# Sliding-window attention followed by an MLP: attention of four heads per visit, in 32-row and 32-column tiles of TensorE

## The chip, the cores and the metric

The kernel runs on one core of one Trainium2 chip. The metric is the device time of one execution in microseconds (us); the figure for a kernel is the median of its runs. TensorE is called PE in the profile, VectorE DVE, ScalarE ACT, GpSimd POOL and SyncE SP.

## What is computed

```python
B, H, S, D = 8, 8, 576, 64; window = 64
scores = q @ k.T / sqrt(D)                    # per batch and head
mask = (rel >= 0) & (rel < window)            # rel = query position - key position
attn = exp(scores - max) / sum, masked; O = attn @ v
x = O of all heads side by side: 4608 tokens x 512
h = x @ w_in (512 x 2048); g = h * sigmoid(h); out = g @ w_out (2048 x 512)
```

Inputs and output are float32 in DRAM; the kernel computes in bf16 with float32 sums. Every query sees at most 64 keys, so a block of 64 queries needs 128 keys: its own block and the one before.

## The kernel before

The 4608 tokens are 72 blocks of 64, nine in each batch, and 9 MLP tiles of 512 tokens. For a tile the first layer (L440) makes 16 blocks of 128 hidden channels, each from four matmuls of 512 columns into one of four PSUM banks `mp`; ACT applies silu (L446) into `g`. The second layer (L449) makes four output blocks of 128 tokens, each from 16 matmuls; ACT or DVE copies them out (L455) and SP stores them (L459).

Attention works on pairs of heads and three blocks at a time: 96 groups, twelve in each batch. `qbd` holds q transposed, the two heads of a pair block-diagonally, so that one matmul with 128 rows of k makes the scores of both heads (`scores`, L349; 3 matmuls of 128 columns). ACT takes the exponential (`expo`, L367), DVE multiplies by a 0/1 mask (`masking`, L370), `values` (L375) multiplies by v with a column of ones for the sum, DVE takes reciprocals (L381) and normalises (L387, L404, L410). O must then be turned so that channels lie on partitions (`bridge`). In the first batches PE does this (`back_both` L420, `back` L431) with a copy (`to_bridge` L436); later DMA does (`turn_o`, L425). q and k are turned by PE in the first batches (`turn_heads` L299, `turn_twos` L308, copied by `lift_q` L321, `lift_k` L327, `lift_twos` L314), later by DMA transposes (`turn_rows` L260) with `spread_q` (L268) for q. `load_v` (L272) loads v for blocks 0 to 127, 128 to 255 and so on; `shift_v` (L335, L337) makes the copy that is shifted by 64 rows. Attention has the four PSUM banks `at`; two buffers each hold q, k and v of a batch.

The order of instructions on each engine is fixed before the kernel runs by the class `Plan`. It plays the program with a duration for each step, and each engine takes the ready step of the lowest rank. MLP matmuls have rank 99, so PE does attention whenever it is ready and MLP matmuls in between; `scores_may_run` holds scores back to the second layer. Idle PE time ahead of the first MLP matmul is filled with matmuls on `ident` (L680). SP carries the first two loads of q and k, the DMA transposes and the stores; POOL carries all other loads.

Of the kernel before, what the change touches and what calls it, by code (L numbers as in the profile page):

```python
# [14 lines left out]
class Plan:  # L15
# [5 lines left out]
    def __init__(self, pools, rank, rank0, ahead):  # L21
        self.rank, self.rank0, self.pools = rank, {**rank0, **{c + "0": r for c, r in ahead.items()}}, pools
        self.queues = {}
        self.banks = [[] for _ in range(8)]
        self.count = 0
        self.now = 0.0

    def add(self, cls, us, fn, deps=(), lat=0.08, gate=None, dma=None, pool=None, table=None, b=0):
        if b > 1 and cls in ("cast", "lift", "spread", "mask", "norm"):
            lat = 0.2  # L30
        op = dict(us=us, first=self.rank[cls] + b if b or cls not in self.rank0 else self.rank0[cls], fn=fn, deps=[d for d in deps if d is not None], lat=lat, gate=gate, dma=dma,
                  pool=pool, table=table, seen=None, n=self.count, until=[], bank=None)
        self.count += 1
        self.queues.setdefault(cls, []).append(op)
        return op

    def add_filler(self, n, cls, us, fn, *args, **kw):

        for _ in range(n):
            op = self.add(cls, us, None, *args, **kw)  # L40
            op["until"], op["fn"] = [op], lambda e, op=op: fn(op)
        self.count -= n

# [3 lines left out]
    def run(self):  # L47
# [4 lines left out]
        table, left = "exp", self.count  # L52
        pipe = {True: 0.0, False: 0.0}
        events, order = [0.0], []
        while left:
# [6 lines left out]
            while moved:  # L62
                moved = False
                for e in engines:
# [3 lines left out]
                    for c in can[e]:  # L68
                        q = self.queues[c]
                        if head[c] == len(q):  # L70
                            continue
                        op = q[head[c]]
                        if e not in op["us"] or (best and best[0]["first"] <= op["first"]):
                            continue
                        if not self.done(op["deps"]) or (op["gate"] and not op["gate"]()):
                            continue
                        if op["pool"] and not any(self.done(self.banks[i]) for i in self.pools[op["pool"]]):
                            continue
                        best = (op, c)
# [3 lines left out]
                    if op["pool"]:  # L83
                        banks = self.banks
                        op["bank"] = min((i for i in self.pools[op["pool"]] if self.done(banks[i])),
                                         key=lambda i: max([u["seen"] for u in banks[i]], default=0.0))
                        banks[op["bank"]] = op["until"]
                    head[c] += 1
                    us = op["us"][e]
                    if op["table"] and op["table"] != table:  # L90
                        table, us = op["table"], us + 1.28
                    end = free[e] = now + us
                    if op["dma"] is None:
                        op["seen"] = end + op["lat"]
                    else:

                        soft = e == "POOL"
                        begin = max(pipe[soft], end + 0.9)
                        pipe[soft] = begin + op["dma"] * (1.25 if soft and pipe[False] > begin else 1.0)
                        op["seen"] = pipe[soft] + 2.2 + (0.0 if now < 40 else 6.0 if soft else {"xk": 5.0, "xo": 1.0}.get(c, 0.0))  # L100
                    op["at"], op["cls"], op["by"] = now, c, e
                    order.append((op, e))
                    left -= c != "warm"
                    moved = True
                    heapq.heappush(events, end)
                    heapq.heappush(events, op["seen"])
        for op, e in order:
            op["fn"](e)
# [3 lines left out]
def kernel(ctx, tc, q, k, v, w_in, w_out, out):  # L112
# [4 lines left out]
    NP = H // 2  # L117
    NB = S // 64
    NM = 6
    NR = S // NM  # L120
    NG = 3
    NDC = d_model // 128
    NFT = d_ff // 128
    TT = 512
    NTT = B * S // TT
    TB = TT // 64
    NK = 2
    NN, NNB, NE, NOB, NOT, NGT = 8, 8, 14, 6, 4, NFT + 3
    PARTS = {0: [(0, 192), (192, TT)]}
    NXQ, NXK, NXO = 4, 2, 3  # L130
    NRAW, NOX, NRC = 2, 2, 12
    NIV, NPM = 2, 1
    scale = 1.0 / float(D) ** 0.5


    ctx.enter_context(tc.manual_schedule())

# [3 lines left out]
    ident = keep.tile([128, 128], BF16, name="ident")  # L141
    twoi = keep.tile([128, 64], BF16, name="twoi")
    zero = keep.tile([128, NP], FP32, name="zero")
    spare = keep.tile([128, NP], FP32, name="spare")
    window = keep.tile([128, 64], BF16, name="window")
    mask0 = keep.tile([128, 3, 2, 64], BF16, name="mask0")
    mask = keep.tile([128, 3, 2, 64], BF16, name="mask")
    bias0 = keep.tile([128, 3, 2, 64], BF16, name="bias0")
    bias = keep.tile([128, 3, 2, 64], BF16, name="bias")
    nats = [keep.tile([NR, 2, NM, 128], BF16, name=f"nat{i}") for i in range(NN)]  # L150
    natbs = [keep.tile([NR, 2 * NM * D], BF16, name=f"natb{i}") for i in range(NNB)]
    qbd = [keep.tile([128, NP, 2, S], BF16, name=f"qbd{i}") for i in range(NK)]
    kt = [keep.tile([128, 64 + NP * S], BF16, name=f"kt{i}") for i in range(NK)]
    vv = [keep.tile([128, H * NB + 1, D + 2], BF16, name=f"vv{i}") for i in range(NK)]
    es = [keep.tile([128, 3, 2, 64], BF16, name=f"e{i}") for i in range(NE)]
    rcs = [keep.tile([128, 3, 2], FP32, name=f"rc{i}") for i in range(NRC)]
    obs = [keep.tile([128, 3, 128], BF16, name=f"ob{i}") for i in range(NOB)]
    raws = [keep.tile([128, 2, S], BF16, name=f"raw{i}") for i in range(NRAW)]
    oxs = [keep.tile([128, 3, NP, 128], BF16, name=f"ox{i}") for i in range(NOX)]
    gts = [keep.tile([128, TT], BF16, name=f"g{i}") for i in range(NGT)]  # L160
    ots = [keep.tile([128, d_model], FP32, name=f"ot{i}") for i in range(NOT)]
    bridge = keep.tile([128, B * NB, NDC, 64], BF16, name="bridge")
    w_in_sb = keep.tile([128, NDC, d_ff], BF16, name="w_in_sb")
    w_out_sb = keep.tile([128, NFT, d_model], BF16, name="w_out_sb")
    banks = [psum.tile([128, 512], FP32, name=f"at{i}") for i in range(4)]
    banks += [psum.tile([128, 512], FP32, name=f"mp{i}") for i in range(4)]

    p = Plan(
        {"at": range(4), "mp": range(4, 8), "all": range(8)},
        rank=dict(prime=-8, one=-9, first=-9, dma=-1, ld0=-1, ld1=-1, st=-2, xo=-1.5, xk=-1.4, silu=-3, out=-2, pv=0, ot=0, s=1, moe=99, warm=200, turn=2,  # L170
                  norm=0, inverse=0, bridge=0, exp=1, mask=1, lift=2, spread=2, shift=2, cast=4, late=5, clear=9),
        rank0=dict(turn=-6, cast=-6, lift=-5, shift=-4.5, exp=-4, mask=-4, inverse=-3.5, norm=-3, bridge=-3.2),
        ahead=dict(s=-5.5, exp=-4.6, pv=-5.5, inverse=-4.3, norm=-4.2, ot=-5.5, bridge=-4.25),
    )
    copies = {"ACT": nc.scalar.copy, "DVE": nc.vector.tensor_copy, "POOL": nc.gpsimd.tensor_copy}
    queue = {"SP": nc.sync, "ACT": nc.scalar, "POOL": nc.gpsimd}


    def const_ident(_):
        nc.gpsimd.memset(ident, 0.0)  # L180
        nc.gpsimd.affine_select(out=ident, in_=ident, compare_op=ALU.not_equal, fill=1.0,
                                base=0, channel_multiplier=1, pattern=[[-1, 128]])

    def const_window(_):

        nc.gpsimd.memset(window, 0.0)
        nc.gpsimd.affine_select(out=window, in_=window, compare_op=ALU.is_ge, fill=-32768.0,
                                base=-1, channel_multiplier=1, pattern=[[-1, 64]])
        nc.gpsimd.affine_select(out=window, in_=window, compare_op=ALU.is_ge, fill=-32768.0,
                                base=64, channel_multiplier=-1, pattern=[[1, 64]])  # L190

    def const_bias(_):
        for t in (bias, bias0):
            nc.vector.tensor_copy(out=t.rearrange("p t h i -> p (t h) i"),
                                  in_=window.unsqueeze(1).to_broadcast([128, 6, 64]))
        nc.vector.memset(bias0[0:64, 0], -32768.0)

    def const_mask(_):
        for a, m in ((bias, mask), (bias0, mask0)):
            nc.vector.tensor_scalar(m, a, 1.0 / 32768.0, 1.0, op0=ALU.mult, op1=ALU.add)  # L200

    def const_twoi(_):
        nc.vector.tensor_copy(out=twoi[0:64], in_=ident[0:64, 0:64])
        nc.vector.tensor_copy(out=twoi[64:128], in_=ident[64:128, 64:128])

    def clear_vv(i):
        nc.vector.memset(vv[i][:, :, D:D + 1], 1.0)
        nc.vector.memset(vv[i][0:64, 0, 0:D], 0.0)

    def clear_k(i):  # L210
        nc.vector.memset(kt[i][:, 0:64].bitcast(FP32), 0.0)

    def clear_q(i, hh):
        r = slice(64 - 64 * hh, 128 - 64 * hh)
# [35 lines left out]
    def rows(i):  # L250
        return nats[i]
# [484 lines left out]
```

## Time and profile before

| | |
|---|---|
| runs | 315.54, 315.95, 319.11 us; median 315.95 |
| profiled execution: span | 318.8 us; of the three runs 319.11 fits this span |
| PE busy | 307.9 us (97%), 2198 matmuls |
| DVE, ACT, POOL busy | 154.5, 193.4, 119.2 us |
| first MLP matmul | starts at 22.1 us |
| software DMA (POOL's queue) | 95712 packets, 18.06 MB |
| hardware DMA (SP's queue) | 42368 packets, 19.08 MB |

A span runs from the first to the last instruction. A line of the timeline gives start, duration, engine, line, operation, tiles written and read, shape and count; lines that overlap on PE are pipelined matmuls, so the distance between the starts of two lines is what the first of them cost. In the view by stages each engine has its busy time and, in brackets, its instructions; then come the granted TensorE clock, the busy share of the DMA engines and the rate of the bytes written. A line of the chain gives start, duration and what the time was spent on.

### The profile page before, as it was taken

To read this page: it belongs to the slowest core of one execution; us is meant where nothing else is said; L and a number is where in the kernel's file an instruction comes from. 1 tells how busy PE (TensorE), PEld (TensorE's weight loads), DVE (VectorE), ACT (ScalarE), POOL (GpSimd) and SP (SyncE) were. 2 spreads that over 40 slices of the span, in tenths; PEclk is the share of its full clock that TensorE was granted. 3 is DMA by queue.
4 is the path that set the end of the run, shared out by engine and by line. 5 is a ranking of instruction groups with operands and counts; after the bars stand their busy time and mean duration, and the time that the engine had idled before them with its cause. 6 is when DMAs were issued, how large, how long until landed. Compare 5 with 4: busy or idle time off the path is not lost.

```text
span 318.8 us, 6010 instructions
## 1 busy us (share of the span) xinstructions
PE 307.9 (97%) x2198; PEld 168.4 (53%) x2223; DVE 154.5 (48%) x467; ACT 193.4 (61%) x374; POOL 119.2 (37%) x159
## 2 busy tenths in 40 slices
PE   8999999999999999999999869999999999999996
PEld 4778666545664556445544445446544444444444
DVE  4894748934799898923990159606920000000000
ACT  8898786889776565568356721668166126415611
POOL 8947859496829777564454000000000000000000
PEclk9999999999999999999999979999999999999999
DMA  9999999999999999999999933400340020020012
GB/s 144 164 196 186 193 195 161 127 243 129 187 165 135 176 154 152 163 163 163 154 191 175 142 64 90 84 0 36 80 93 2 35 97 0 2 99 33 2 61 70
DMA packets 138108, 37.51 MB, mean 118 GB/s; under 512 B 122464, under 2 KB 133600, under 8 KB 138080
## 3 DMA queue, kind: packets, MB, share of 16 engines
q0 software_dynamic: 95712, 18.06, 74.4%
q1 hardware_dynamic: 42368, 19.08, 33.6%
q8 instruction: 17, 0.28, 0.4%
q14 instruction: 11, 0.09, 0.1%
HBM read 36.70 MB, written 9.44 MB: 145 GB/s over the span
## 4 chain that ended last, share of the span: by engine, by line
PE 85%; DVE 6%; DMA 4%; issue 2%; ACT 1%; POOL 1%; DVEq 0%; POOLq 0%; ACTq 0%
PE mp L449 36%; PE mp L440 32%; PE at L375 5%; PE at L349 4%; DMA vv<-in_v_dram 4%; DVE qbd L314 2%; PE at L680 1%; PE mp L680 1%; DVE ox L404 1%; POOL vv L272 1%; DVE qbd L268 1%; DVE vv L337 1%; DVE vv L335 1%; PE at L308 1%; PE at L420 1%
## 5 line engine op out<-in xcount | busy, mean ns | idle before, releaser
L449 PE MATMUL mp<-w_out_sb,g 128*128 128x512 bf16 (+2 forms) x583 | 141.6, 369 | 1.0
L440 PE MATMUL mp<-bridge,w_in_sb 128*128 128x512 bf16 (+2 forms) x640 | 130.7, 358 | 0.7 <-ACT g L446 0.6
L446 ACT ACTIVATE g<-mp 128x512 bf16<-128x512 f32 (+2 forms) x160 | 86.3, 556 | 29.8 <-PE mp L440 29.3
L440 PEld LDWEIGHTS <-w_in_sb 128*128 128x128 bf16 x640 | 60.1, 98 | 60.3 <-issue 1.4
L449 PEld LDWEIGHTS <-g 128*128 128x128 bf16 x608 | 55.0, 98 | 42.7
L455 ACT COPY ot<-mp 128x512 f32<-128x512 f32 (+2 forms) x34 | 19.0, 561 | 72.1 <-PE mp L449 62.7
L404 DVE TENSOR_TENSOR ox<-at,rc 64x192 bf16<-64x192 f32 x128 | 45.2, 353 | 2.5
L254 POOL DMA_DIRECT2D nat<-in_k_dram x48 | 36.4, 761 | 24.3 <-DMA nat<-in_k_dram 13.0
L367 ACT ACTIVATE e<-at 128x384 bf16<-128x384 f32 x90 | 38.8, 497 | 10.6 <-PE at L349 9.8
L370 DVE TENSOR_TENSOR e<-e,mask 128x384 bf16<-128x384 bf16 x84 | 26.6, 350 | 33.6 <-ACT e L367 32.8
L272 POOL DMA_DIRECT2D vv<-in_v_dram x32 | 32.3, 1014 | 13.1 <-PE at L375 7.2
L375 PE MATMUL at<-vv,e 128*128 128x130 bf16 x273 | 29.8, 220 | 4.1 <-DVE e L370 4.0
L375 PEld LDWEIGHTS <-e 128*128 128x128 bf16 x288 | 22.5, 97 | 20.0 <-DVE e L370 7.6
L254 POOL DMA_DIRECT2D nat<-in_q_dram x32 | 23.4, 735 | 8.1 <-DMA nat<-in_q_dram 4.6
L349 PEld LDWEIGHTS <-kt 128*128 128x128 bf16 x252 | 18.6, 100 | 10.0 <-issue 2.8
L349 PE MATMUL at<-qbd,kt 128*128 128x128 bf16 x252 | 23.6, 222 | 0.3
L381 DVE RECIPROCAL rc<-at 128x6 f32<-128x6 f32 x91 | 17.5, 194 | 10.1 <-PE at L375 8.0
L314 DVE COPY qbd<-at 64x288 bf16<-64x288 bf16 x26 | 12.5, 480 | 11.1 <-ACT qbd L314 7.6
L387 DVE TENSOR_TENSOR ob<-at,rc 64x192 bf16<-64x192 f32 x40 | 14.0, 350 | 0.8
L314 ACT COPY qbd<-at 64x288 bf16<-64x288 bf16 x22 | 10.5, 476 | 2.8 <-DVE qbd L314 2.5
L268 DVE COPY qbd<-raw 64x1152 bf16<-64x1152 bf16 x16 | 8.1, 505 | 8.4 <-DMA raw<-nat 8.0
L235 POOL DMA_DIRECT2D natb<-in_q_dram x15 | 10.0, 665 | 4.9 <-PE at L375 1.4
(69 smaller groups left out, 158.0 us busy)
## 6 DMA issues: line engine op xcount, KB each, us to landing
out_dram<-ot SPq DMA_DIRECT2D x35, 256.0 KB, 2.4
vv<-in_v_dram POOLq DMA_DIRECT2D x32, 144.0 KB, 7.3
nat<-in_k_dram POOLq DMA_DIRECT2D x48, 72.0 KB, 7.9
nat<-in_q_dram POOLq DMA_DIRECT2D x32, 72.0 KB, 7.6
natb<-in_q_dram POOLq DMA_DIRECT2D x15, 144.0 KB, 6.4
w_in_sb<-in_moe_w_in_dram POOLq DMA_DIRECT2D x8, 256.0 KB, 8.7
w_out_sb<-in_moe_w_out_dram POOLq DMA_DIRECT2D x8, 256.0 KB, 7.8
natb<-in_k_dram POOLq DMA_DIRECT2D x7, 144.0 KB, 5.9
```

The source lines that it names most:

```text
L254: nc.gpsimd.dma_start(out=rows(i)[:, pj % 2, :, 64 * hh:64 * hh + 64], in_=(q, k)[kk][b, 2 * pj + hh].rearrange("(m p) d -> p m d", p=NR),)
L272: queue[e].dma_start(out=vv[b % NK][:, 2 * g0 + 1:2 * g1 + 1:2, 0:D], in_=v[b].rearrange("h s d -> (h s) d").rearrange("(g p) d -> p g d", ...
L314: copies[e](out=qbd[b % NK][64 * hh:64 * hh + 64, pj, hh].rearrange("x (p m) -> x p m", m=NM)[:, :, r::2], in_=at_bf16(op)[64 * r:64 * r + ...
L349: nc.tensor.matmul(at_sp(op)[:, x], lhsT=kt[b % NK][:, pj * S + t * 64:pj * S + t * 64 + 128], rhs=qbd[b % NK][:, pj, :, t * 64:t * 64 + 6 ...
L367: nc.scalar.activation(out=es[n % NE], in_=at_sp(op), func=ACTF.Exp, scale=scale)
L370: nc.vector.tensor_mul(es[n % NE], es[n % NE], mask0 if g == 0 else mask)
L375: nc.tensor.matmul(at_pv(op)[:, x], lhsT=es[n % NE][:, x].rearrange("p h i -> p (h i)"), rhs=vv[b % NK][:, s:s + NB + 1:NB, 0:D + 1], star ...
L404: nc.vector.tensor_mul(ox(n)[:, :, r], pv[r, :, hh, 0:D], rc[r, :, hh:hh + 1].to_broadcast([64, 3, 64]))
L440: nc.tensor.matmul(banks[bank["bank"]][:, lo:hi], lhsT=w_in_sb[:, c, ft * 128:(ft + 1) * 128], rhs=bridge[:, (j * TT + lo) // 64:(j * TT + ...
L446: nc.scalar.activation(out=gts[gt][:, lo:hi], in_=banks[bank["bank"]][:, lo:hi], func=ACTF.Silu)
L449: nc.tensor.matmul(banks[bank["bank"]][:, 0:hi - lo], lhsT=gts[gt][:, m * 128:(m + 1) * 128], rhs=w_out_sb[:, f, lo:hi], start=(f == 0), s ...
L455: copies[e](out=ots[ot][:, lo:hi], in_=banks[bank["bank"]][:, 0:hi - lo])
```

## The change

Attention is written anew; the MLP keeps its shape. Four heads are handled at once, one in each quarter of the 128 partitions. Within a quarter, a 32-partition strip holds 32 of the head's 64 channels at a time: a row of q or k is seen as 32 words of two bf16 numbers, and DVE turns 32x32 blocks of such words (`turn`). The channel pairs then lie next to each other, and scores sum over the two members (`r`) in two matmuls with 32 rows each, at row tile 32j for head j, each head into a PSUM bank of its own. `values` takes 32 queries as weights, at column tile 32j, so that 32 queries of four heads fill the 128 partitions of a bank. After reciprocal and `norm`, DVE turns 32x32 blocks of O straight into `bridge` (`cross`), which has its channels in a new order; `load_w_in` loads w_in's rows in that order. All transposes on PE and by DMA go.

A visit is the attention of up to eight blocks for one group of four heads (`quad`): 64 matmuls for scores, two exps and two masks, 64 matmuls for values, reciprocal, norm, cross. It uses four PSUM banks at once (`A`), first for the scores, then for the values. The nine blocks of batch 0 are done ahead of the MLP in four smaller visits (blocks 0 to 3 and 4 to 8 of each group), with all eight banks. After that the two visits for tile j+1 are placed within the second layer of tile j (`may_score`). The first layer's first two pieces have 256 and 320 columns. q and k of batch 0 come as float32 in 16 loads on SP and are cast by ACT and DVE; all other loads are on POOL, with three buffers for q, k and v. The planner is a shorter one with new ranks and durations. Parts of the diff (the removed functions are those printed above):

```diff
-    banks = [psum.tile([128, 512], FP32, name=f"at{i}") for i in range(4)]
-    banks += [psum.tile([128, 512], FP32, name=f"mp{i}") for i in range(4)]
+    half = [psum.tile([128, 4, 512], FP32, name="at"), psum.tile([128, 4, 512], FP32, name="mp")]
...
+        {"A": [(0, 1, 2, 3)], "AD": [(0, 1, 2, 3), (4, 5, 6, 7)], "D": [(i,) for i in range(4, 8)],
+         "any": [(i,) for i in range(8)]},
+        rank=dict(one=-9, cast=-2, turn=2, shift=3, scores=-1, exp=0, mask=1, values=-2, inverse=-1, norm=0, cross=0.5,
+                  prime=-8, silu=-3, out=4, moe=99, warm=200, load=0, first=0, st=1),
+        rate=0.37,
...
+    def rows(x, b, h):
+        return x[b, h].rearrange("(t p m) d -> p t (m d)", p=32, m=2)
+    def load_wide(i, x, quad, j):
+        nc.sync.dma_start(out=wide[i][32 * j:32 * j + 32], in_=rows(x, 0, 4 * quad + j))
+    def load_rows(w, x, b, quad, j):
+        nc.gpsimd.dma_start(out=raws[w][32 * j:32 * j + 32], in_=rows(x, b, 4 * quad + j))
+    def load_v(b, i):
+        n = min(128, S - 128 * i)
         nc.gpsimd.dma_start(
+            out=vas[b % NK][0:n, i, :, 0:D], in_=v[b, :, 128 * i:128 * i + n].rearrange("h p d -> p h d"))
...
+    def turn(w, b, quad, kk, lo, hi):
+        t = kts[b % NK][:, quad, 64:] if kk else qts[b % NK][:, quad]
+        nc.vector.transpose(
+            out=t.rearrange("x s c -> x (s c)").bitcast(FP32)[:, 64 * lo:64 * hi].rearrange("x (t p m) -> x t m p", p=32, m=2),
+            in_=raws[w][:, lo:hi].rearrange("p t y -> p (t y)").bitcast(FP32).rearrange("p (t m x) -> p t m x", m=2, x=32))
+
+    def shift_v(e, b, up):
+        a, z = vas[b % NK], vbs[b % NK]
+        if up:
+            copies[e](out=z[64:128, :, :, 0:D], in_=a[0:64, :, :, 0:D])
...
+    def scores(op, quad, blocks):
+        ps = half[op["bank"][0] // 4]
+        for s, g in enumerate(blocks):
+            b, t = divmod(g, NB)
+            for r in range(2):
+                for j in range(4):
+                    x = slice(32 * j, 32 * j + 32)
+                    nc.tensor.matmul(
+                        ps[:, j, 64 * s:64 * s + 64], lhsT=kts[b % NK][x, quad, 64 * t:64 * t + 128, r],
+                        rhs=qts[b % NK][x, quad, 64 * t:64 * t + 64, r], start=(r == 0), stop=(r == 1),
+                        tile_position=(32 * j, 0))
+    def expo(op, n, j0, j1, nb):
+        nc.scalar.activation(out=es[n % NE][:, j0:j1, 0:64 * nb], in_=half[op["bank"][0] // 4][:, j0:j1, 0:64 * nb],
+                             func=ACTF.Exp, scale=scale)
+    def masking(n, j0, j1, nb):
+        t = es[n % NE][:, j0:j1, 0:64 * nb].rearrange("k j (s i) -> k j s i", i=64)
+        nc.vector.tensor_mul(t, t, mask.unsqueeze(1).unsqueeze(1).to_broadcast([128, j1 - j0, nb, 64]))
+    def values(op, n, quad, blocks):
+        ps = half[op["bank"][0] // 4]
+        for s, g in enumerate(blocks):
+            b, t = divmod(g, NB)
+            vv = (vas if t % 2 else vbs)[b % NK][:, t // 2]
+            for a in range(2):
+                for j in range(4):
+                    x = slice(32 * j, 32 * j + 32)
+                    c = (2 * (s % 2) + a) * (D + 1)
+                    nc.tensor.matmul(
+                        ps[x, s // 2, c:c + D + 1], lhsT=es[n % NE][:, j, 64 * s + 32 * a:64 * s + 32 * a + 32],
+                        rhs=vv[:, 4 * quad + j, 0:D + 1], start=True, stop=True, tile_position=(0, 32 * j))
...
+    def norm(op, n, nb):
+        for lo, hi, ps in pieces(op, nb):
+            kk = ps.shape[1]
...
+    def cross(n, quad, g0, nb):
+        nc.vector.transpose(
+            out=bridge[:, 2 * quad:2 * quad + 2, 64 * g0:64 * (g0 + nb)].rearrange("x c (u i) -> x c u i", i=32),
+            in_=obs[n % NO][:, 0:2 * nb].rearrange("i u (x c) -> i c u x", c=2))
...
+        op, kind, rest = moe[may_score.i]
+        return (kind == 1 and rest == NF * NC and not p.done(op["deps"])) or (kind == 2 and rest > 8)
...
+        s = p.add("scores", {"PE": 0.1 + 0.11 * nb}, None, need, lat=0.15, pool="AD" if early else "A",
+                  gate=None if early else may_score)
...
+        for j0, j1 in ([(0, 4)] if early else [(0, 2), (2, 4)]):
+            ex = p.add("exp", {"ACT": 0.2 + 0.000834 * 64 * nb * (j1 - j0)}, lambda _, j0=j0, j1=j1: expo(s, n, j0, j1, nb),
+                       [s] + e_free.get(n - NE, []), table="exp")
+            ma.append(p.add("mask", {"DVE": 0.16 + 0.00053 * 64 * nb * (j1 - j0)}, lambda _, j0=j0, j1=j1: masking(n, j0, j1, nb),
+                            [ex, c_mask]))
+            exps.append(ex)
+            s["until"].append(ex)
+        va = p.add("values", {"PE": 0.1 + 0.11 * nb}, None, ma + [x for g in blocks for x in v_done[g]], lat=0.15,
+                   pool="AD" if early else "A")
...
+        rc = p.add("inverse", {"DVE": 0.25}, lambda _: inverse(va, n, nb), [va])
+        no = p.add("norm", {"DVE": 0.2 + 0.134 * nb}, lambda _: norm(va, n, nb), [rc] + o_free.get(n - NO, []))
+        va["until"].append(no)
+        cr = p.add("cross", {"DVE": 0.1 + 0.134 * nb}, lambda _: cross(n, quad, blocks[0], nb), [no])
+        o_free[n] = [cr]
...
+    for quad in range(2):
+        for lo, hi in FIRST:
+            add_visit(quad, list(range(lo, hi)), early=True)
+    add_qk(1)
+    add_v(1)
...
+    add_first([(64 * lo, 64 * hi) for lo, hi in FIRST], "any")
+    loaded = 1
+    for j in range(NT):
+        if j + 1 < NT:
+            lo = NB if j == 0 else 8 * (j + 1)
+            blocks = list(range(lo, 8 * (j + 2)))
+            while loaded < blocks[-1] // NB:
+                loaded += 1
+                add_qk(loaded)
+                add_v(loaded)
+            for quad in range(2):
+                add_visit(quad, blocks)
+        add_second(j)
+        if j + 1 < NT:
+            add_first([(64 * blocks[0], 64 * blocks[-1] + 64)], "D")
```

## The prediction

> **What bounds the kernel now.** I read the busy shares first, then the chain of work that ended last, then busy time by stage, then the timeline of TensorE (PE).
>
> ```profile
> PE 307.9 (97%) x2198; PEld 168.4 (53%) x2223; DVE 154.5 (48%) x467; ACT 193.4 (61%) x374; POOL 119.2 (37%) x159
> ...
> PE 85%; DVE 6%; DMA 4%; issue 2%; ACT 1%; POOL 1%; DVEq 0%; POOLq 0%; ACTq 0%
> ```
>
> PE is 97% busy and is 85% of the chain, so a microsecond of PE work is a microsecond of time wherever nothing else is late. The long pieces of the chain give the price of the MLP:
>
> ```profile
> 131.69 13.81 PE mp L440 x64
> ...
> 171.67 12.93 DMA vv<-in_v_dram
> ...
> 260.39 13.81 PE mp L440 x64
> ...
> 302.10 13.64 PE mp L449 x94
> ```
>
> 64 matmuls of 512 columns take 13.81 us, 215.8 ns each; the 1152 of both layers take 248.6. Smaller pieces of the first tile and of the last store add 0.6: 249.2. They start at 22.1 and end near 315.5, and the store ends the span at 318.8. So 318.8 = 22.1 (opening) + 249.2 + 3.3 (tail) + 44.2 (all else). The DMA line is part of that: v of a late batch lands at 184.6, and PE sits idle:
>
> ```profile
> 185.99 0.51 PE L375 MATMUL at<-vv,e 128*128 128x130 bf16 x3 [4.00 <-DVE e L370]
> ...
> 178.00:201.00 23.00, 18.83 (x120) 10.17 (x122) 14.05 (x45) 7.83 (x16) 0.00 (x0) 0.93 0.68 93
> 215.00:233.00 18.00, 17.84 (x131) 10.13 (x132) 13.36 (x45) 8.66 (x18) 0.00 (x0) 1.00 0.27 67
> ```
>
> The last two lines are the same stage (second layer plus its attention groups) with and without the late v; the third figure from the right is the granted TensorE clock. It is 0.93 of full in the first: after the idle 4.0 us, 0.07 x 23 = 1.6 us more were lost to a lower clock. So 5.6 of the 44.2 is this stall and 38.6 is attention on PE: scores and values of 84 groups about 28 (0.17 us for three matmuls each), transposes of q, k and O about 7, small waits the rest.
>
> **Its own time.** The three runs are 315.54, 315.95 and 319.11. A span of 318.8 fits only the last, 0.3 more than the span; the median is 3.2 below it, so I take it that the stall is smaller in the others.
>
> **What goes.** The PE transposes and their evacuations, the DMA transposes of q, k and O, and the diagonal layout of q go: about 7 us of PE between 22 and 62. DMA gets lighter: 80 loads of 576 packets become 32 to 33 thousand packets of twice the size, and all transposing packets (most of the 42368 hardware ones) go. Three buffers instead of two hold k and v. I therefore count the v stall at nothing; the cover is that a batch is loaded in some 12 us of DMA (10 thousand packets, at the 9 to 10 thousand per 10 us moved here between 70 and 120) out of a 35 us stretch. POOL issues 16 loads x 0.73 and 5 x 1.01 = 17 us per batch, also inside 35. If that cover failed, the 5.6 would be back.
>
> **What PE gets.** A visit (8 blocks, 4 heads) has two PE stages, scores and values, of 64 matmuls each with 64 or 65 moving columns, as 16 sets of four tiles. 63 blocks x 2 head groups / 8 = 15.75 visits lie after the opening. The nearest rows:
>
> ```profile
> 20.64 0.38 PE L420 MATMUL mp<-ident,ox 128*64 128x64 bf16 x12
> 20.95 0.35 PE L375 MATMUL at<-vv,e 128*128 128x130 bf16 x3
> 21.22 0.28 PE L420 MATMUL mp<-ident,ox 128*64 128x64 bf16 x6
> 21.44 0.34 PE L375 MATMUL at<-vv,e 128*128 128x130 bf16 x3
> ...
> 46.54 0.25 PE L431 MATMUL at<-twoi,ob 128*128 128x64 bf16 x3
> 46.63 0.38 PE L449 MATMUL mp<-w_out_sb,g 128*128 128x512 bf16 x1
> ```
>
> L420 works in pairs of 64-column tiles. Twelve take 20.95 - 20.64 = 0.31 us, six take 0.22: three more pairs cost 0.09, so a pair costs 30 ns, as much as one full-width matmul of L431 (0.09 / 3). Two column tiles thus do run side by side. The rest, 0.22 - 0.09 = 0.13, is the way out of the tile shape; the way in shows as 0.26 before L420 at 14.15 where three matmuls take 0.17: 0.09. Together 0.21 per stage, hidden by nothing.
>
> Four tiles, and row tiles at all, no row shows. Below: a set goes like a pair, 30 ns. Above: it goes like two pairs, 60 ns, which is also 8 instructions at the 7.5 ns that the pair shows. I take the middle, 45, since the pair is near both: a stage is 0.21 + 16 x 0.045 = 0.93, a visit 1.86, all 29.3 us (21.7 to 37.0 at the ends). Before, a steady second-layer stage with its groups takes 17.1 (from 146.0 to 163.1); after it is 13.8 + 4 x 0.93 = 17.5. The steady tile gains nothing; the gain is the transposes, the stall, and that q, k and O need no PE in the first three tiles.
>
> The Trainium skill's page "TensorEngine Tiling (Array Packing)", section Restrictions and Gotchas, speaks against this: column tiles lose the fast weight load. With an estimate from "TensorE: Matmul & The Clock Gate", section LDWEIGHTS (columns / 1.2 ns), four 32-column loads in a row would be 107 ns a set and the sum some 16 us higher. L420's loads are tiled too, and its pair still costs 30 ns, so I go by the row.
>
> **What DVE and ACT get.** ACT: 512 columns take 0.60, 192 take 0.31, so 1024 (half a visit's exp) take 1.06. DVE: PSUM multiplies of 384 and 192 columns take 0.541 and 0.353, 0.98 ns an element and 0.17 fixed; a norm of 1024 is 1.17. A mask of 384 takes 0.350, so 1024 take 0.66. The 32x32 transpose has no row. Below, a dense copy: 1152 in 0.51. Above, the dearest DVE element here, 353 / 192 = 1.84 ns: 1.9 for 1024. I take one element per 0.98 ns, as any unaided DVE pass here: cross 1.17, a turn of 576 words 0.73. Per tile of 31 us DVE gets some 12 and ACT 18, so neither is the bound by its sum.
>
> **The chain inside a tile.** Both visits of the next tile must end within one second-layer stage, because one PSUM half carries both stages of both. From its start: scores to 0.9; last silu and table load to 2.0; two exps to 4.1; mask 4.9; values 5.1 to 6.0; reciprocal 6.4; norm 7.7; scores of the second visit 7.9 to 8.8; exps 11.1; mask 11.9; values 12.0 to 13.0; reciprocal 13.3; norm 14.6; cross 15.9. PE reaches the first layer at 17.5, so 1.6 are spare. Where a step is late, PE stands at values or at the first layer's first matmul, the MLP matmuls queued behind wait with it, and silu and the stores wait for those. The order is fixed ahead at 0.98 us for a stage, so a quicker PE comes early to values and waits; I give 2 us in all.
>
> **Opening.** SP issues 16 loads of q and k at 0.41 from 0.74, until 7.3; five v loads (1.01 each) start once the first k has landed, about 5.3. That is 3.5 MB of reads at 0.30 to 0.38 MB per us (the first and second 10 us here): v lands near 13.5. Two shifts (0.79 and 0.86 now for 2304) to 15.2; values 0.7; then reciprocal, norm and cross of three small visits, 5.2 us of DVE, before both head groups have blocks 0 to 3: 21.5 to 22.5. I take 22.0 (19 to 25): nothing gained on 22.1. Casts and turns come before v lands.
>
> **Sum.** 22.0 + 249.2 + 29.3 + 2.0 + 3.3 = 305.8 span, 306.1 with the 0.3. That is 13 below the profiled run and 3.1% below the median of 315.95. About 2% (309.6 to 322.3) is what a measurement here can tell from no change.
>
> **Rivals.** (1) The chain outlasts the stage. If transposes cost 1.9 and the broadcast mask goes at 0.98 ns an element (1.17), and a turn stands in the way once per visit, the chain is 3 us longer: 1.4 over in each of 8 stages, 11 us, and with the 2 already counted 315. It decides from 1.6 us on. For it: one PSUM half, single visits in flight; against: DVE is idle for most of the first-layer stage, where turns fit. The page "VectorE: DVE Perf Modes", section The three transpose paths, gives 311 ns for a 128x128 bf16 transpose; scaled, an estimate of 2.5 for a cross, it would add 1.3 to the chain, just inside the spare time. No run here shows it.
> (2) Slower: tiles do not overlap in one of the stages. Row tiles write four PSUM banks at once and read every second element; no row shows either. At 30 ns a matmul the stage is 0.21 + 1.92 = 2.13; for scores alone 15.75 x 1.20 = 19 more, 325; for both, 344. It decides at 2.9 us a visit, 77 ns a set. Against: L420's pairs.
> (3) Better: 30 ns a set and no waits, 22.0 + 249.2 + 21.7 + 3.6 = 296.5.
>
> **How the numbers follow.** Forecast with its own range 297 to 313: 0.67 (0.58 of it under 309.6). Rival 1: 0.14 (0.02 faster, 0.10 within 2%, 0.02 slower). Rival 2: 0.13, all slower. Rival 3 exactly or below: 0.03. A late opening or a new DMA wait of 5 us or more: 0.03, within 2%. That makes faster 0.63, same 0.22, slower 0.15. The range 297 to 321 leaves out rival 2 and the best cases, under 2 in 10.
>
> **What would show it.** Right: both PE stages at 0.7 to 1.2 us with sets of four starting within nanoseconds; first MLP matmul near 22; tiles 31 to 32 us apart; no wait of PE for v. Wrong: single matmuls 30 ns apart in the tiled stages; PE waiting at the first layer for cross; DVE transposes well above 1.2 us; a first MLP matmul after 25.

## The result, and the profile after

The changed kernel takes 469.69 us (four runs, 466.74 to 473.14) against 316.23 for the kernel before: a ratio of 1.486, 95% interval 1.474 to 1.497. The forecast was 306.1 with a range of 297 to 321. The kernel got slower by half where it was to get a little faster, and the forecast was 163.6 us too low. (Some executions of the kernel before last about 5 us longer than its others; medians are over all runs, ratios and intervals are those on record, and against the shorter executions of before alone, 314.8 to 317.9, the ratios of e1 and of e5 to e9 below would be 0.005 to 0.015 higher.)

The page of the changed kernel, its span being 467.1 us: busy time, the granted TensorE clock in 40 slices (9 is full speed), and the chain that ended last by engine and by line. L275 and L288 are the two MLP layers, L283 is silu, L292 the copy out. The last line is that of the first layer in the table of groups: busy us, mean ns of one, and after the second bar the time that PE idled before these matmuls and what ended most of it.

```profile
PE 324.7 (70%) x3588; PEld 150.0 (32%) x3631; DVE 115.8 (25%) x179; ACT 161.2 (35%) x244; POOL 115.4 (25%) x175
...
PEclk9799999799999999999999999999769999999999
...
PE 61%; ACT 23%; DMA 6%; issue 6%; POOL 2%; DVE 1%; another core or an unknown queue 1%; ACTq 0%; DVEq 0%; POOLq 0%
PE mp L275 30%; PE mp L288 24%; ACT gate L283 18%; ACT ot L292 4%; DMA va<-in_v_dram 4%; PE at L288 3%; DMA w_in_sb<-in_moe_w_in_dram 2%; PE at L275 2%; PE at L223 2%; PE at L245 1%; POOL va L187 1%; DVE ot L292 1%; POOL raw L183 1%; ACT L283 1%
...
L275 PE MATMUL mp<-bridge,w_in_sb 128*128 128x512 bf16 (+3 forms) x552 | 144.6, 380 | 93.1 <-ACT gate L283 86.1
```

PE fell from 97% to 70% busy, and ACT, which was 1% of the chain, is 23%. It does less work than before (161.2 us against 193.4), yet it ends waits: 18% of the span is silu. No engine is the bound by its sum. The view of waits says who stands for whom (total us, times, longest):

```profile
PE mp L275 <- ACT gate L283: 86.1, 128, 0.9
...
PE mp L288 <- ACT ot L292: 11.7, 17, 0.7
```

One stage in the timeline shows the pattern (start, duration, engine and line; in brackets the idle time before and what ended it):

```profile
338.24 1.86 PE L275 MATMUL mp<-bridge,w_in_sb 128*128 128x512 bf16 x4 [0.68 <-ACT gate L283]
340.79 1.86 PE L275 MATMUL mp<-bridge,w_in_sb 128*128 128x512 bf16 x4 [0.68 <-ACT gate L283]
...
347.68 0.60 ACT L283 ACTIVATE gate<-mp 128x512 bf16<-128x512 f32 x1 [1.84 <-PE mp L275]
348.33 1.02 PE L275 MATMUL mp<-bridge,w_in_sb 128*128 128x512 bf16 x4 [0.68 <-ACT gate L283]
349.39 0.60 ACT L283 ACTIVATE gate<-mp 128x512 bf16<-128x512 f32 x1 [1.11 <-PE mp L275]
350.03 1.02 PE L275 MATMUL mp<-bridge,w_in_sb 128*128 128x512 bf16 x4 [0.69 <-ACT gate L283]
351.09 0.60 ACT L283 ACTIVATE gate<-mp 128x512 bf16<-128x512 f32 x1 [1.11 <-PE mp L275]
```

PE and ACT take turns: four matmuls, 1.06 us later silu, 0.60 for silu, 0.05 to the next matmul. A group takes 1.71 us (350.03 - 348.33 is 1.70) where four matmuls at 215.8 ns make 0.86. There are four banks, so a group should wait only for silu of the group four earlier; here it waits for the group just before. The first two lines are the same at half the granted clock (0.50 from 333.7 to 347.4): 2.55 us a group.

Summed over the trace, from the start of each MLP piece to the start of PE's next work, the MLP takes some 400 us: 252 in the first layer, 148 in the second. The prediction had 249.2 for both. That is some 151 too much, nearly the whole miss of 161.3 in the span (467.1 - 305.8).

### The profile page after: what moved, and what is told of

Same layout as the page of the kernel before. It is cut to its first block, busy times and chain, and to the rows that moved or that the text cites. A ratio compares the mean times of both kernels' runs of the same rounds, so it can differ in the third digit from the quotient of the medians.

```text
span 467.1 us, 8158 instructions
## 1 busy us (share of the span) xinstructions
PE 324.7 (70%) x3588; PEld 150.0 (32%) x3631; DVE 115.8 (25%) x179; ACT 161.2 (35%) x244; POOL 115.4 (25%) x175
## 2 busy tenths in 40 slices
DMA packets 86275, 29.50 MB, mean 63 GB/s; under 512 B 72672, under 2 KB 81760, under 8 KB 86240
## 4 chain that ended last, share of the span: by engine, by line
PE 61%; ACT 23%; DMA 6%; issue 6%; POOL 2%; DVE 1%; another core or an unknown queue 1%; ACTq 0%; DVEq 0%; POOLq 0%
PE mp L275 30%; PE mp L288 24%; ACT gate L283 18%; ACT ot L292 4%; DMA va<-in_v_dram 4%; PE at L288 3%; DMA w_in_sb<-in_moe_w_in_dram 2%; PE at L275 2%; PE at L223 2%; PE at L245 1%; POOL va L187 1%; DVE ot L292 1%; POOL raw L183 1%; ACT L283 1%
## 5 line engine op out<-in xcount | busy, mean ns | idle before, releaser
L275 PE MATMUL mp<-bridge,w_in_sb 128*128 128x512 bf16 (+3 forms) x552 | 144.6, 380 | 93.1 <-ACT gate L283 86.1
L288 PE MATMUL mp<-w_out_sb,gate 128*128 128x512 bf16 (+1 forms) x514 | 116.3, 369 | 22.1 <-ACT ot L292 11.7
L283 ACT ACTIVATE gate<-mp 128x512 bf16<-128x512 f32 (+3 forms) x141 | 80.9, 574 | 146.5 <-PE mp L275 139.4
L275 PEld LDWEIGHTS <-w_in_sb 128*128 128x128 bf16 x640 | 63.1, 99 | 190.1 <-issue 144.6
L288 PEld LDWEIGHTS <-gate 128*128 128x128 bf16 x608 | 56.2, 97 | 82.2 <-issue 23.4
L234 DVE TENSOR_TENSOR e<-e,mask 128x1024 bf16<-128x1024 bf16 (+2 forms) x36 | 24.8, 688 | 132.2 <-ACT e L229 132.0
L187 POOL DMA_DIRECT2D va<-in_v_dram x40 | 34.8, 888 | 71.7 <-PE at L245 70.8
L229 ACT ACTIVATE e<-at 128x1024 bf16<-128x1024 f32 (+1 forms) x33 | 31.6, 1008 | 30.4 <-PE at L223 30.3
L292 ACT COPY ot<-mp 128x512 f32<-128x512 f32 (+1 forms) x27 | 15.2, 562 | 74.3 <-PE mp L288 48.0
L183 POOL DMA_DIRECT2D raw<-in_k_dram x56 | 34.0, 622 | 16.5 <-DVE rc L259 10.1
L183 POOL DMA_DIRECT2D raw<-in_q_dram x56 | 34.8, 633 | 11.5 <-DMA va<-in_v_dram 5.6
L269 DVE STREAM_TRANSPOSE bridge<-o 128x1024 bf16<-128x1024 bf16 (+3 forms) x20 | 22.4, 1124 | 0.4
L275 PE MATMUL at<-bridge,w_in_sb 128*128 128x256 bf16 (+1 forms) x76 | 12.4, 285 | 7.0 <-ACT gate L283 6.4
L288 PE MATMUL at<-w_out_sb,gate 128*128 128x512 bf16 (+1 forms) x63 | 12.7, 352 | 2.2 <-ACT ot L292 2.1
```

The lines of the kernel that those rows point to most:

```text
L183: nc.gpsimd.dma_start(out=raws[w][32 * j:32 * j + 32], in_=rows(x, b, 4 * quad + j))
L187: nc.gpsimd.dma_start(out=vas[b % NK][0:n, i, :, 0:D], in_=v[b, :, 128 * i:128 * i + n].rearrange("h p d -> p h d"))
L229: nc.scalar.activation(out=es[n % NE][:, j0:j1, 0:64 * nb], in_=half[op["bank"][0] // 4][:, j0:j1, 0:64 * nb], func=ACTF.Exp, scale=scale)
L234: nc.vector.tensor_mul(t, t, mask.unsqueeze(1).unsqueeze(1).to_broadcast([128, j1 - j0, nb, 64]))
L269: nc.vector.transpose(out=bridge[:, 2 * quad:2 * quad + 2, 64 * g0:64 * (g0 + nb)].rearrange("x c (u i) -> x c u i", i=32), in_=obs[n % NO ...
L275: nc.tensor.matmul(bank(bk["bank"][0])[:, 0:hi - lo], lhsT=w_in_sb[:, c, ft * 128:(ft + 1) * 128], rhs=bridge[:, c, lo:hi], start=(c == 0) ...
```

## The experiments

**Theory A.** The cause is the line `half = [psum.tile([128, 4, 512], ...), psum.tile([128, 4, 512], ...)]`. Four banks are one tile there, and waits are kept for the tile as a whole: whoever writes one bank waits for the reader of another. In the order of the program 152 of the 159 first-layer groups that follow another lie in the same tile as it, and none in the same bank. The rivals: attention is what takes the time (tiles that don't overlap, a visit's chain that is too long), or the loads, or the banks themselves, or the stretches at half clock.

**e1_banks.** The second half is four tiles of one bank each; nothing else of the method changes. Early visits, which also use these banks, take one exp and one norm per bank there.

```diff
-    half = [psum.tile([128, 4, 512], FP32, name="at"), psum.tile([128, 4, 512], FP32, name="mp")]
+    half = psum.tile([128, 4, 512], FP32, name="at")
+    single = [psum.tile([128, 512], FP32, name=f"mp{i}") for i in range(4)]
...
-         "any": [(i,) for i in range(8)]},
+         "any": [(i,) for i in range(4, 8)]},
```

Expected:

> The changed kernel with one edit: the second PSUM half is four tiles of one bank each instead of one tile of four banks (early visits that use it take one exp and one norm per bank), and the first MLP pieces keep to these four. Theory A: waits are kept per tile, so a first-layer group in one bank waits for the silu of the group before in another bank; then the 144 waits of 0.6 us on silu go, a first-layer stage falls from some 27 us to 14, a second-layer stage loses its waits on the copies, and the time falls by about 150 us: opening 36 + MLP 249 + visits 26 + tail and waits 7 = 318 (308 to 330). Rival B: four banks are too few beside visits that hold the other four, and the waits are for the bank's own reader: no change, 455 to 475. Rival C: the granted clock at half for some 30 us is the cause: no change either, since nothing of the clock is edited.

Measured: 313.07 us (four runs, 311.99 to 315.45), ratio 0.983 (0.971 to 0.995). Its page, busy time and the two MLP groups (busy, mean ns, and after the second bar the idle time before them):

```profile
PE 294.8 (94%) x3623; PEld 149.0 (47%) x3623; DVE 116.3 (37%) x184; ACT 159.9 (51%) x246; POOL 115.8 (37%) x175
...
L297 PE MATMUL mp<-w_out_sb,gate 128*128 128x512 bf16 (+2 forms) x608 | 129.7, 368 | 0.0
L284 PE MATMUL mp<-bridge,w_in_sb 128*128 128x512 bf16 (+3 forms) x640 | 126.8, 358 | 0.0
```

The 93.1 us that PE idled ahead of the first layer (the line of L275 above) are 0.0. One line of allocation is 157 us. With it mended the new attention is no slower than the old: beside e1's 311.99 to 315.45, six runs of the kernel before took 315.08 to 317.85, so the gain is nearer 1% than the 1.7% of the ratio.

**e2_before_one.** The converse, in the kernel before: only its four MLP banks become one tile.

```diff
-    banks += [psum.tile([128, 512], FP32, name=f"mp{i}") for i in range(4)]
+    mp = psum.tile([128, 4, 512], FP32, name="mp")
+    banks += [mp[:, i] for i in range(4)]
```

Expected:

> The kernel before with one edit: its four mp banks are one tile of four banks. Theory A: each first-layer group (0.86 us) now also waits for the silu before it (0.6) and two hand-overs of some 0.1: 0.8 x 144 = 115 us more, and the second layer's first matmul waits for a copy (0.6 + 0.2, 36 times, part of it hidden): 430 to 470 in all. Rivals B and C: the banks and their number are as before: 316.

Measured: 509.01 us (502.35 and 515.68), beyond the range. The first layer's group in this kernel's table of groups:

```profile
L441 PE MATMUL mp<-bridge,w_in_sb 128*128 128x512 bf16 (+2 forms) x640 | 176.0, 400 | 104.0 <-ACT g L447 97.7 <-ACT ot L456 5.2 <-DVE ot L456 0.8
```

The stall is the same with the old attention: 97.7 us of waiting for silu. It needs nothing of the new attention. The surplus over the expectation stands beside two things that the expectation left out: a longer time at half clock, 88.2 us of this span of 500.6 (openings included) against 33.1 in the changed kernel and 5.5 before, and a first MLP matmul at 31.1 instead of 22.1. How much each is worth was not separated.

**e5_twin_adjacent and e6_twin_apart.** Is it the tile, or something of the banks? Both are e1 with the four banks in two tiles of two, and differ in which banks share a tile. By their numbers in the program the banks are used in the same cycle in both as in e1 (1, 2, 3, 0). Where in PSUM each number lies is not on record.

```diff
-    single = [psum.tile([128, 512], FP32, name=f"mp{i}") for i in range(4)]
+    twin = [psum.tile([128, 2, 512], FP32, name=f"mp{i}") for i in range(2)]
+    single = [twin[i // 2][:, i % 2] for i in range(4)]     # e5: banks 0,1 and 2,3
+    single = [twin[i % 2][:, i // 2] for i in range(4)]     # e6: banks 0,2 and 1,3
```

Expected of e5:

> The kernel with tiles of one bank (313 us), with the four banks now in two tiles of two banks, the banks used one after the other in one tile. Order and banks are the same; 79 of 159 first-layer groups and 19 of 38 second-layer groups now follow a group in the same tile (152 and 36 in the changed kernel). Theory A, waits per tile: each of these waits some 0.85 us more (the silu of 0.6 and its hand-overs), 79 x 0.85 + 19 x 0.8 = 82: about 395 (375 to 415). Rival: one tile of four is special, or the reuse of a bank is what is waited for: 313.

Expected of e6:

> As the run with two tiles of two banks, but the banks of one tile are used two groups apart: no group follows one in its own tile. Theory A: a group waits for the silu of the group two before, which is over 0.8 us after that group's end, while the group between takes 0.86; next to nothing is lost: 313 to 322. Rival (any tile of more than one bank costs, by its size): as the adjacent pairs.

Measured: e5 384.07 us (383.77, 384.37), ratio 1.203 (1.192 to 1.214); e6 323.92 (323.85, 323.99), ratio 1.015 (1.005 to 1.024). The view of waits, first of e5, then of e6:

```profile
PE mp L285 <- ACT gate L293: 42.6, 66, 0.9
```

```profile
PE mp L285 <- ACT gate L293: 4.9, 8, 0.9
```

Counting in the order of the program how many first-layer groups follow a group in their own tile gives 152 of 159 in the changed kernel, 79 in e5 and none in e6 and e1. Half as many, half the waiting (42.6 against 86.1 us); none, almost none. e5 also answers the rival of the clock: behind its opening it runs at full clock throughout, and still takes 71 us more than e1. e6 came slightly above its range, 10.9 us above e1: with two banks to a tile, silu has one group's time to be done instead of three, and where ACT also has an exp to do that is short. That last reading is argued, not shown.

**e3_open and e4_banks_open.** The second miss is the opening: the first MLP matmul starts at 36.41 us instead of 22. The timeline of the changed kernel:

```profile
1.51 4.33 POOL L187 DMA_DIRECT2D va<-in_v_dram  x5
...
5.78 2.12 POOL L191 DMA_DIRECT2D w_in_sb<-in_moe_w_in_dram  x3
...
7.88 4.99 SPq L180 DMA_DIRECT2D gate<-in_q_dram  x4
...
25.95 0.76 DVE L200 CAST raw<-gate 128x1152 bf16<-128x1152 f32 x1 [5.30 <-DMA gate<-in_q_dram]
...
36.41 1.22 PE L275 MATMUL at<-bridge,w_in_sb 128*128 128x256 bf16 x8
```

POOL issues v at 1.51 and w_in from 5.78, ahead of SP's last four loads of q. "v after the first k has landed" was an entry in the planner and no wait in the program. The last q, issued between 7.88 and 12.9, is cast only at 25.95. That the loads ahead of it are the cause is what the next runs ask. e3 is the changed kernel, and e4 is e1, with one addition: POOL reads a word of each of the four q and k tiles before it issues w_in.

```diff
+    def landed_all(_):
+        for i in range(4):
+            nc.gpsimd.tensor_copy(out=seen[:, i:i + 1], in_=wide[i][96:128, NB - 1, 0:1])
```

Expected of e3:

> The changed kernel with one edit: POOL reads one word of each float32 q and k tile of batch 0 before it issues the loads of w_in, so that w_in does not share the DMA engines with them. Theory A for the opening (it is late because v and w_in are moved ahead of the second group's q, which is cast only at 26): q is cast near 14, the first MLP matmul starts at 24 to 28 instead of 36.4, and the time falls by 8 to 12, to 455 to 460. Rival: the opening is bound by the landing of v and by DVE: first MLP matmul stays near 36 and the time at 467.

Expected of e4:

> Both edits, tiles of one bank and the late w_in. Theory A: the two causes add: 318 - 10 = 308 (297 to 320), near the 306 that was predicted. Rival: with PE no longer held back, the chain of a visit inside a second-layer stage is the bound and 8 stages grow by 2 us or more: 320 to 330.

Measured: e3 462.67 us (466.13, 459.22, of which one lies in the expected range), first MLP matmul at 29.75; e4 317.88 (ten runs, 315.84 to 320.96), ratio 1.004 (1.000 to 1.009), first MLP matmul at 30.5. Both openings became shorter, by 6.7 and 4.4, so the order of the loads is part of the cause, but they miss the 24 to 28 that was expected, and in e4 the gain was lost again: its time lies in its range, but 4.8 above e1, so the two edits do not add. w_in left later, so w_out arrived later, and the second layer of the first tile stood for it (timeline of e4):

```profile
50.75 5.08 PE L302 MATMUL mp<-w_out_sb,gate 128*128 128x512 bf16 x15 [3.37 <-DMA w_out_sb<-in_moe_w_out_dram]
```

The second tile starts at 70.2 in e4 and at 68.7 in e1, the third at 105.0 and 99.0; what is lost between these two was not followed up. Here, holding one load back moved the wait to a later one.

**e7_k_on_pool, e8_long_rows, e9_long_rows_k_pool, e10_one_load.** Four versions of e1 that change the loads. e7 brings k of batch 0 by POOL, as bf16 and ahead of v. e8 gives each partition 18 whole rows, 4608 bytes in one piece, instead of 9 pieces of 512 (packets in all fall from 86275 to 53507). e9 is both. e10 is e9 with one load for a group of four heads instead of four loads.

```diff
 # e8
-        return x[b, h].rearrange("(t p m) d -> p t (m d)", p=32, m=2)
+        return x[b, h].rearrange("(p m) d -> p (m d)", p=32)
 # e10
-        nc.gpsimd.dma_start(out=raws[w][32 * j:32 * j + 32].rearrange("p t y -> p (t y)"), in_=rows(x, b, 4 * quad + j))
+        nc.gpsimd.dma_start(out=raws[w].rearrange("p t y -> p (t y)"),
+                            in_=x[b, 4 * quad:4 * quad + 4].rearrange("h (p m) d -> (h p) (m d)", p=32))
```

Expected of e7:

> The kernel with tiles of one bank, with k of batch 0 loaded on POOL as bf16 ahead of v and w_in (no float32 copy, no cast), q on SP as before. Theory A for the opening (the second group's q and k share the DMA engines with v and w_in, ahead of which they should be): first MLP matmul at 25 to 30 instead of 34.9; the later loads come some 5 us later, and the second layer of tile 0 may wait for w_out: 305 to 313 in all. Rival: bytes and packets through w_out are the bound of the first 70 us whatever their order: 311 to 317.

Expected of e8:

> The kernel with tiles of one bank, and every load of q and k in 32 pieces of 4608 bytes a head (18 rows to a partition) instead of 288 of 512; the DVE transpose writes with a stride of 18 words, so the result is the same. Theory D: the first 130 us are bound by DMA, by the number of pieces and not by their order (putting k first gave 10 us at the start and lost them by the third tile): 32 thousand pieces go, the MLP starts at 27 to 32 and the third tile at 88 to 95 instead of 99: 302 to 308. Rival: bytes are the bound, or v's 256-byte pieces are: 311 to 316.

Expected of e9:

> Both: long pieces, and k of batch 0 ahead on POOL. Theory D: the early start (25.0 with short pieces) is now kept through the third tile: 298 to 305. Rival: 311 to 316, as either alone.

Expected of e10:

> As the run with long pieces and k on POOL, with one load on POOL for the four heads of a group (128 pieces of 4608 bytes) in place of four loads: 4 instead of 16 issues a batch, at some 0.6 us each, the same bytes and pieces. Theory P: POOL's issue time, 16 to 18 of each 20 us until 140, is what is left of the bound on the loads; then the start comes near 25 and the third tile near 90: 300 to 306. Rival D: bytes on the DMA engines are (some 160 GB/s written, twice that read, in every stretch until 140): 309 to 312, no change.

| | median us (runs) | ratio, interval | first MLP matmul | third tile starts |
|---|---|---|---|---|
| e1 | 313.07 (4) | 0.983, 0.971 to 0.995 | 34.9 | 99.0 |
| e7 | 313.50 (5) | 0.981, 0.974 to 0.989 | 25.0 | 98.6 |
| e8 | 312.44 (4) | 0.984, 0.965 to 1.003 | 29.8 | 97.1 |
| e9 | 311.35 (4) | 0.979, 0.966 to 0.992 | 28.3 | 95.9 |
| e10 | 306.89 (6) | 0.974, 0.970 to 0.977 | 25.3 | 92.2 |

e7 starts 9.9 us earlier than e1 and by the third tile has 0.4 of it left: the first two tiles wait for what the opening pushed back, and the time is that of the rival. Long pieces alone (e8) give nothing that can be told from e1, so e8 and e9 missed, and the rival of both held. e8 is not the number of packets alone, though: its DVE transposes of 576 words take 1.25 us instead of 0.76, and DVE is busy for 129.9 us instead of 116.3. e10 is the fastest kernel of this study, 2.6% below the kernel before, and 0.9 above its range. Its one edit against e9 is that one load takes the place of four. POOL's busy time by stretches (start:end, length, busy us and instructions of PE, PEld, DVE, ACT, POOL, then granted clock, DMA share, GB/s), first e9, then e10:

```profile
60.00:80.00 20.00, 19.75 (x244) 9.96 (x231) 13.96 (x16) 14.97 (x23) 16.56 (x29) 1.00 1.37 170
100.00:120.00 20.00, 20.00 (x277) 9.56 (x275) 13.23 (x17) 13.17 (x20) 17.10 (x29) 1.00 1.23 140
```

```profile
60.00:80.00 20.00, 19.76 (x282) 10.14 (x280) 16.73 (x19) 15.54 (x25) 4.25 (x6) 1.00 1.12 156
100.00:120.00 20.00, 18.69 (x330) 9.22 (x329) 11.79 (x16) 10.52 (x14) 1.17 (x3) 1.00 0.54 89
```

POOL falls from 17 of 20 us to 4 and 1, but these stretches are not where most of the gain lies: 3.0 of the 3.9 us by which the span shrank (308.7 to 304.8) are there at the first MLP matmul. That POOL's queue sets the order there is read from the traces, not tested apart. The issue of the first v, in the timeline of e9 and in that of e10:

```profile
6.11 2.86 POOL L188 DMA_DIRECT2D va<-in_v_dram  x3
```

```profile
2.52 0.92 POOL L189 DMA_DIRECT2D va<-in_v_dram  x1
```

Eight issues of k stand ahead of v in e9 and two in e10, so v starts 3.6 us earlier. What still keeps the opening of e10 above 22 is the landing of v (9.03 us of its chain, from 5.94) and the DVE work behind it; which loads v shares the time with was not tried.

## Why the prediction was wrong

**The step that failed** is the term "MLP 249.2": 1152 matmuls at 215.8 ns, taken over unchanged, with "2 us in all" for waits. It measured some 400, because PE waited for silu of the group before in nearly every first-layer group, and likewise for the copies out in the second layer. I had read from the diff that attention uses four banks at once, and asked what that does to attention ("one PSUM half carries both stages of both" visits). I did not ask what the same line does to the other half, where the MLP's banks went into one tile as well. The line stood in the diff, with minus signs in front of the eight one-bank tiles that it replaced. The price was in the trace of before: 0.60 for silu and 0.05 to 0.1 of hand-over, against a group of 0.86. A group that waits for its predecessor's silu takes 1.71 and not 0.86; 152 x 0.85 = 129 us, and the first layer measured 252 - 124.6 = 127 more. (The agreement is partly luck: shorter groups cost less than 0.85, and the stretches at half clock add.) The second layer's 36 like groups wait some 0.7 each for the copy out, 25; it took 23 more.

None of the rivals had it. The one that ended slower put the loss into tiles that don't overlap, 325 to 344. Its mechanism is refuted by the 30 ns a set below, and the failure was elsewhere.

**Opening 22.0** measured 36.4 (34.9 in e1), outside its 19 to 25. The working let v start after k and let SP's 16 loads go at their issue rate; the order on POOL was that of the program, and v, w_in and q shared the DMA engines. **The 0.3 around the span** was wrong too: the profiled execution of the changed kernel took 468.91 for a span of 467.1, 1.8 more, and e1's 315.45 for 313.7. So the profiled execution of before, with its span of 318.8, was none of the three runs. By the same 1.8 the median run of before has a span of some 314.1, an estimate, so most of the 5.6 that the sum gained on the late v was not there to gain.

**What held** is seen in e1, where the MLP is as before. Its timeline holds two attention stages, scores (L224) and values (L249):

```profile
58.56 0.25 PE L249 MATMUL at<-vb,e 128*32 128x65 bf16 x8
58.62 0.25 PE L249 MATMUL at<-va,e 128*32 128x65 bf16 x8
...
58.92 0.26 PE L249 MATMUL at<-vb,e 128*32 128x65 bf16 x8
...
181.01 4.06 PE L297 MATMUL mp<-w_out_sb,gate 128*128 128x512 bf16 x18
185.00 0.68 PE L224 MATMUL at<-qt,kt 32*128 32x64 bf16 x64
185.62 1.69 PE L297 MATMUL mp<-w_out_sb,gate 128*128 128x512 bf16 x7
```

From 58.56 to 58.92 are six steps of eight matmuls, 0.06 each: a set of four tiles takes 30 ns, the low end of what I allowed and a full overlap. Between 181.01 and 185.62 lie 18 MLP matmuls (3.88) and one stage of scores, 0.73 with the way in and out; predicted 0.93, low end 0.69. If values cost the same, a visit takes about 1.45 us of PE and 15.75 visits 22.8. e1's span adds up as 34.9 + 249.2 + 22.8 + 3.1 (tail) with 3.7 left for waits, against the 31.3 that I gave visits and waits together. With 12.9 more of opening and 4.8 less of attention the sum would have been 313.9, where e1's span is 313.7.

The chain inside a tile was not put to the test as I had written it, because the order on PE does not keep two visits inside one second layer. From e1's timeline (L284 is its first layer):

```profile
96.01 0.69 PE L224 MATMUL at<-qt,kt 32*128 32x64 bf16 x64
96.62 2.55 PE L297 MATMUL mp<-w_out_sb,gate 128*128 128x512 bf16 x11
99.01 1.03 PE L284 MATMUL mp<-bridge,w_in_sb 128*128 128x512 bf16 x4
99.96 0.24 PE L249 MATMUL at<-vb,e 128*32 128x65 bf16 x8
```

Scores stand at the end of a second layer and the values of the same visit in the next first layer. Visits run ahead, so the second layers from 241.3 on hold none, and tiles start 27.6 to 34.7 us apart where 31 to 32 was forecast.

DVE's prices held as well. The transposes of O and of q and k in the changed kernel, each shape by itself:

```profile
L269 DVE STREAM_TRANSPOSE bridge<-o 128x1024 bf16<-128x1024 bf16 x14 | 17.3, 1233 | 0.3
...
L204 DVE STREAM_TRANSPOSE kt<-raw 128x576 f32<-128x576 f32 x14 | 10.6, 755 | 21.3 <-PE at L223 21.3
```

1.23 and 0.76 us were predicted as 1.17 and 0.73. Rival 1's dear transposes (1.9) are gone with them.

Two rules were weighed in the prediction and both now have a number. The Trainium skill's page "TensorEngine Tiling (Array Packing)", section Restrictions and Gotchas, has column tiles lose the fast weight load; here a set of four column tiles with its four loads takes 30 ns, so the estimate of 107 built on that does not hold for loads of 32 columns. The estimate of 2.5 us for a cross, scaled from the page "VectorE: DVE Perf Modes", section The three transpose paths, was twice the measured 1.23.

## What to carry to other kernels

When buffers are regrouped, price the waits that go with the grouping, for every user of the buffers and not only for the one that the change is about: a write to one bank of a shared tile waited here for the reader of another, 0.85 us in each of 152 groups. The sign is quick to find in a profile: two engines strictly in turn, and idle time that one line ends a hundred times by the same amount. The page "PSUM — Partial Sum Buffer", section PSUM bank collisions raise a hardware error, asks for semaphores by bank and quadrant, by bank in its simple version; a guard over four banks cost 157 us here, and with two banks to a tile it depended on which two (384 against 324).

## What the runs showed that I had not expected

Where PE waits briefly again and again, the granted clock can fall to half. Two stretches of the changed kernel and one of e1 (columns as above):

```profile
330.00:350.00 20.00, 13.19 (x34) 4.01 (x33) 0.00 (x0) 5.97 (x10) 0.00 (x0) 0.66 0.00 0
350.00:467.00 117.00, 80.22 (x364) 34.64 (x370) 0.00 (x0) 29.43 (x51) 0.00 (x0) 1.00 0.07 27
```

```profile
40.00:313.00 273.00, 268.23 (x3225) 132.82 (x3223) 96.95 (x132) 146.95 (x226) 89.97 (x133) 1.00 0.64 84
```

From 330 to 350 PE does nothing but first layer, waits 0.68 us after every four matmuls, and has a mean clock of 0.66: 2 x 0.34 x 20 = 14 us at half. Behind it the same pattern runs at 1.00. Beyond the openings the changed kernel spends some 20 us at half clock, e2 some 78 and e1 none; but e5, where PE waits for silu 66 times, also has none. The Trainium skill's page "TensorE: Matmul & The Clock Gate", section A second HAM failure mode: psum-queue depth-cycling, tells of this: small idles between groups of matmuls that go round PSUM banks let the clock swing between half and full. The traces of the changed kernel and of e2 agree, and give the size of the idles; e5 and the stretch behind 350 show that such idles alone do not decide it. What starts and ends such a stretch stays open.

The SBUF tile `gate` is also written by silu in slices while PE reads other slices, and shows no such wait in e1 (0.0 us of idle ahead of L297; at 241.35 the second layer reads `gate`, and silu still writes another slice of it at 241.55), so a shared tile does not always serialise. Why the two differ was not tried.
